# Batch 1's values half pooled on VectorE, five normalisations on ScalarE, and a new order of steps in a pooled-attention and MLP-mixer kernel

## The chip, the cores and the metric

The kernel runs on one core of a Trainium2 chip. The core has a matrix engine (TensorE, in the profile PE, with its weight loads as PEld), a vector engine (VectorE, DVE), a scalar engine (ScalarE, ACT), GpSimd (POOL) and SyncE (SP), which work side by side, each through its own instructions in order, and wait for each other by semaphores. TensorE writes its products to PSUM, from where DVE or ACT fetches them. The metric is the time of one execution on the device in microseconds (us), median of several runs.

## The reference

Attention over pooled keys and values, then an MLP mixer. There are 8 batches, 8 heads, 576 positions, 64 elements a head.

```python
k_p = k.reshape(B, H, 72, 8, D).mean(axis=3)        # 8 neighbours pooled: 72 keys
v_p = v.reshape(B, H, 72, 8, D).mean(axis=3)
scores = scale * q @ k_p^T                          # 576 x 72 a head
attn = exp(scores) / sum(exp(scores))
x = (attn @ v_p), heads side by side                # (8, 576, 512)
h = relu(x^T @ w_tok1) @ w_tok2                     # 576 -> 256 -> 576
u = x + h^T
out = u + relu(u @ w_ch1) @ w_ch2                   # 512 -> 1536 -> 512
```

## The kernel before

The kernel is one long program whose order is written out by hand. HEAD is a string of steps that load and compute batch 0 up to the mixer's input. PLAN has a dictionary for each of nine **units**. A unit n is the channel MLP (w_ch1, relu, w_ch2, sum) of the first 512 rows of batch n; the ninth (n = 8) does the remaining 64 rows of all eight batches together. A unit is a generator (unit_fast) that stops 45 times, at steps 0 to 44, each after about 0.44 us of matmuls; PLAN says which steps of the later batches are put in at each stop. So the MLP of batch n and the attention of batches n+1 to n+3 share TensorE.

The steps of a batch b are written "b.name" (functions in batch_steps):
- lk, lq, lv load the keys, queries and values (POOL's DMA queue); s0 to s2 compute scores and their exponentials (TensorE, then ACT).
- K0, K1 and V0, V1 pool half of the keys or values by three additions on POOL (pool8, L173 to L183). k0, k1, v0, v1 do the same on DVE, vpool0 and vpool1 by eight identity matmuls on TensorE (ppool, L261) and a copy.
- Q0, Q1 transpose the queries (DVE); kpT transposes the pooled keys on TensorE, with a copy on ACT.
- av0 to av4 multiply the exponentials with the values for one block of rows (TensorE, L388), take the reciprocal of the sums (DVE, L392) and normalise: one multiplication on DVE (L331). With on_act, named aw0 to aw4, the reciprocal stays on DVE and the normalisation is eight ACT multiplications, one a head, each with a scale of its own per row (L333 to L335).
- at0, at1 are the token MLP's first product, u0 to u4 its second with the sum x + h (L423); t0 to t3 transpose u through TensorE and ACT. From batch 3 on the transposition goes through memory instead: M0, M2, M4 write u out, M and MT read it back in another layout (SP's queue), T0 to T5 transpose blocks on DVE (L465).

Steps without a batch: "=1" to "=4" are sums of parts of the hidden activations GT (g_sums, DVE), w0 to w3 sums of w_ch2 (weight_sum). "g" is a gate: DVE writes a flag (L809) and POOL copies it (L810), so that POOL does not go on to its later loads and poolings before DVE is there. In HEAD, d1 to d4 are dummy matmuls on TensorE, p0 and p1 permute w_tok2 (ACT, POOL), c0 and c1 convert queries, Lxx are loads.

The MLP in a unit. In units 0 to 6 twelve l1_tile calls (L523, two steps each) make GT with a relu on ACT (L530). In units 7 and 8 (FAST) l1_fast makes it in 21 smaller products of three groups A, B, C, seven each, in the order of ORDER; ACT keeps partial products (L621), DVE adds them (L625) and applies the relu (L628). Then seven products of twelve matmuls (product, L680) make the output, each three steps, with additions on DVE (L723). Before the change, in a FAST unit, the first product starts when all 21 are issued and three empty steps have gone by.

PSUM has four banks of one tile, p1a to p1d, handed out in turn (take, give), and two double buffers p2 that scores and av share.

Of the kernel before, what the change touches and what calls it, by code (L numbers as in the profile page):

```python
# [12 lines left out]
ALU = mybir.AluOpType  # L13
# [8 lines left out]
PLAN = [  # L22
# [9 lines left out]
]  # L32

# [2 lines left out]
def kernel(  # L36
# [523 lines left out]

    def g_sums(s, eng):
        S4 = sums_tile("S", "area")
        if s[0] == "3":
            sub(S4[:, 2], GT[:, 0, f], GT[:, 1, f], eng)
        elif s[0] == "1":
            eng.tensor_tensor(out=S4[:, 0], in0=GT[:, 1, f], in1=GT[:, 1, sec], op=ALU.add)
        elif s[0] == "2":
            sub(S4[:, 1], S4[:, 0], GT[:, 0, f], eng)
        else:
            sub(S4[:, 3], GT[:, 0, sec], S4[:, 1], eng)  # L570

    def weight_sum(k):
        T = sums_tile("T", "area2")
# [28 lines left out]
    def l1_fast(n, uT):  # L602
# [20 lines left out]
        def add(g, k, ps, row, half):  # L623
            dst = GT[:, half, row * NH + 2 * g:row * NH + 2 * g + 2]
            nc.vector.tensor_tensor(out=dst, in0=ps, in1=kept[g, k], op=ALU.add)  # L625
            if g > 0:
                dst = GT[:, half, row * NH + 4 * (g - 1):row * NH + 2 * g + 2]
                nc.vector.tensor_scalar(out=dst, in0=dst, scalar1=0.0, scalar2=None, op0=ALU.max)  # L628

        def step(g, k):  # L630
            if k == 1:
                if g > 0:
                    bank[g, 0], bank[g, 1] = (take([P, 2, 256], FP32) for _ in range(2))
                else:
                    bank[g, 0], bank[g, 1] = (ps_two.tile([P, 2, 512], FP32, name="p2")[:, 0].rearrange(
                        "p (j n) -> p j n", j=2) for _ in range(2))
            ps = bank[g, k in (2, 3, 5)]
            a, c = factors[k]
            for j in range(2):
                for kk in range(2):  # L640
                    nc.tensor.matmul(out=ps[:, j], lhsT=a(2 * g + j, kk), rhs=c(kk),
                                     start=k in (1, 2, 5) and j == 0 and kk == 0, stop=kk == 1, skip_group_check=True)
            if k == 1 or k == 5:
                keep(g, k)
            elif k == 6:
                keep(g, 2)
            elif k == 2:
                add(g, 1, ps, 0, 0)
            elif k == 3:
                add(g, 2, ps, 0, 1)  # L650
            elif k == 7:
                add(g, 5, ps, 1, 1)
            else:
                nc.scalar.activation(out=GT[:, 0, NH + 2 * g:NH + 2 * g + 2], in_=ps, func=AF.Relu)
                if g == NM // 4 - 1:
                    for i in range(4):
                        give(bank[1 + i % 2, i // 2])

        return step

    ORDER = "A1 A2 B1 B2 A6 C1 C2 A5 A7 B6 A3 B5 B7 A4 C6 B3 C5 C7 B4 C3 C4"

    def unit_fast(n, u):
        last = n == B
        uT = [u["uT"][:, kk, :] for kk in range(4)]
        if n in FAST:
            step = l1_fast(n, uT)
            for t in ORDER.split():
                step("ABC".index(t[0]), int(t[1]))
                yield  # L670
            for _ in range(3):
                yield
        else:
            for m in range(NM):
                yield from l1_tile(n, m, uT)

        def product(ps, a, w, start, after, split=False, end=None):
            for i in range(2):
                for m in range(NH):
# [45 lines left out]
                    then(e)  # L725
            return go

        def store_part(cols, engines):
            def go(i):
                if len(engines) == 2:  # L730
                    engines[i].dma_start(out=tail_rows(1, cols)[:, i], in_=ob[:, i, cols])
                elif i == 1:
                    engines[0].dma_start(out=tail_rows(1, cols), in_=ob[:, :, cols])
# [4 lines left out]
        x, y = bank(last), bank()  # L738
        s1 = keep("s1")
        yield from product(x, lambda m: GT[:, 0, m], lambda m: w_ch2[:, m, lo], True,  # L740
                           plus(part(s1), part(x), residual(0, 0)), last)
# [142 lines left out]
```

## Time and profile before

| | |
|---|---|
| median of 3 runs | 264.78 us (264.6 to 265.11) |
| the profiled execution | 265.02 us |
| its span, first to last instruction | 263.2 us |
| instructions | 5488 |
| granted TensorE clock, mean | 0.999 |
| HBM read, written | 38.99 MB, 12.58 MB (196 GB/s over the span) |

The span cut at the handovers from one unit to the next, roughly (us of busy time of each engine):

| stretch, us | what | PE | DVE | ACT | POOL |
|---|---|---|---|---|---|
| 24 to 57 | unit 0 | 32.03 | 25.42 | 15.89 | 18.28 |
| 57 to 87 | unit 1 | 29.10 | 22.06 | 19.49 | 28.79 |
| 87 to 115 | unit 2 | 27.63 | 20.48 | 13.06 | 25.31 |
| 115 to 146 | unit 3 | 29.93 | 25.31 | 13.31 | 26.55 |
| 146 to 222 | units 4 to 6 | 75.73 | 52.74 | 33.50 | 46.19 |
| 222 to 241 | unit 7 | 18.87 | 18.38 | 6.86 | 2.98 |
| 241 to 263 | unit 8 and the end | 18.51 | 18.07 | 6.86 | 0.00 |

How to read lines of the timeline: start and length in us, engine, line of the kernel, operation, tile written <- tiles read, shape, how many are merged (x); in brackets the idle time of that engine before it, and what ended it. Starts count from the first instruction. Matmuls are pipelined, so the length of one is more than its spacing to the next: a matmul of 512 columns follows the one before it after 0.216 us, one of 256 after 0.109.

### The profile page before, as it was taken

How to read it: one execution, taken by the hardware profiler on the slowest of the kernel's cores; microseconds unless marked ns; L12 is line 12 of the kernel's file. 1: busy time of each engine (PE TensorE's matmuls, PEld its weight loads, DVE VectorE, ACT ScalarE, POOL GpSimd, SP SyncE). 2: the span in 40 equal slices, each digit the busy share in tenths (PEclk: the TensorE clock that was granted, in tenths of full speed). 3: DMA queues.
4: the chain of work that ended last, by engine and by line, in shares of the span. 5: the costliest groups of instructions: out<-in, count | busy, mean ns of one | idle time of the engine just before them, and what ended most of it. 6: DMA issues, size and time to landing. Idle time of an engine off the chain costs nothing. (4 is left out here: it accounts for less than half of the span.)

```text
span 263.2 us, 5488 instructions
## 1 busy us (share of the span) xinstructions
PE 254.0 (97%) x2171; PEld 167.7 (64%) x2193; DVE 195.7 (74%) x400; ACT 119.0 (45%) x195; POOL 166.1 (63%) x177
## 2 busy tenths in 40 slices
PE   8999999989999999999998999999999999999994
PEld 2785466754667544774476447754684478888883
DVE  3557469986787665896599686863696389999994
ACT  2355763149537466415640565255625421712700
POOL 8667326899999999978879992798407922100000
PEclk9999999999999999999999999999999999999999
DMA  7999999993079928599645932650315052602404
GB/s 148 187 198 207 205 207 208 206 225 75 4 127 145 163 86 168 133 185 249 127 152 94 215 130 66 97 156 1 126 37 161 2 157 63 181 0 49 114 2 159
DMA packets 31706, 34.31 MB, mean 130 GB/s; under 512 B 3136, under 2 KB 23744, under 8 KB 31680
## 3 DMA queue, kind: packets, MB, share of 16 engines
q0 software_dynamic: 17632, 17.64, 42.4%
q1 hardware_dynamic: 13632, 15.93, 20.4%
q8 instruction: 17, 0.28, 0.5%
q10 hardware_dynamic: 416, 0.39, 0.5%
q14 instruction: 9, 0.07, 0.1%
HBM read 38.99 MB, written 12.58 MB: 196 GB/s over the span
## 5 line engine op out<-in xcount | busy, mean ns | idle before, releaser
L526 PEld LDWEIGHTS <-w_ch 128*128 128x128 bf16 x336 | 30.2, 98 | 33.4 <-issue 2.7
L680 PEld LDWEIGHTS <-area 128*128 128x128 bf16 x432 | 41.4, 98 | 7.5 <-issue 1.0
L810 POOL COPY flag<-flag 1x1 f32<-1x1 f32 x41 | 12.5, 304 | 43.1 <-DVE flag L809 43.0
L309 ACT ACTIVATE ex<-p 72x768 bf16<-72x768 f32 x42 | 31.5, 802 | 17.1 <-PE p L300 17.1
L680 PEld LDWEIGHTS <-GT 128*128 128x128 bf16 x324 | 30.7, 98 | 7.5 <-issue 1.6
L178 POOL TENSOR_TENSOR t<-t 72x512 f32<-72x512 f32 x23 | 32.4, 1409 | 1.8
L526 PE MATMUL p1c<-uT,w_ch 128*128 128x512 bf16 x100 | 28.0, 379 | 0.2
L177 POOL TENSOR_TENSOR t<-kr 72x1024 f32<-72x1024 bf16 x12 | 25.5, 2121 | 0.4
L177 POOL TENSOR_TENSOR t<-vr 72x1024 f32<-72x1024 bf16 x11 | 23.4, 2123 | 2.4 <-DMA vr<-in_v_dram 1.9
L331 DVE TENSOR_TENSOR x<-p,den 128x512 bf16<-128x512 f32 x32 | 22.1, 691 | 1.1
L526 PE MATMUL p1b<-uT,w_ch 128*128 128x512 bf16 x75 | 21.3, 379 | 0.4 <-issue 0.2
L530 ACT ACTIVATE GT<-p1c 128x512 bf16<-128x512 f32 x26 | 15.5, 597 | 12.3 <-PE p1c L526 8.5
L526 PE MATMUL p1a<-uT,w_ch 128*128 128x512 bf16 x72 | 20.5, 379 | 0.3
L526 PE MATMUL p1d<-uT,w_ch 128*128 128x512 bf16 x74 | 19.9, 379 | 0.2 <-issue 0.2
L530 ACT ACTIVATE GT<-p1b 128x512 bf16<-128x512 f32 x20 | 11.9, 596 | 15.3 <-PE p1b L526 8.8
L530 ACT ACTIVATE GT<-p1d 128x512 bf16<-128x512 f32 x19 | 11.4, 599 | 14.0 <-PE p1d L526 8.5
L388 PEld LDWEIGHTS <-ex 72*128 72x128 bf16 x280 | 12.9, 98 | 7.5 <-DVE x L331 2.0
L423 DVE TENSOR_TENSOR u<-p1d,x 128x512 bf16<-128x512 f32 x11 | 8.0, 727 | 11.9 <-PE p1d L422 11.0
L554 DVE TENSOR_TENSOR area<-GT 128x1536 bf16<-128x1536 bf16 x9 | 11.4, 1263 | 6.9 <-ACT AT L402 5.2
L388 PE MATMUL p<-vp,ex 72*128 72x65 bf16 x280 | 14.4, 194 | 1.0 <-DVE x L331 0.5
L121 POOL DMA_DIRECT2D kr<-in_k_dram x17 | 10.9, 646 | 5.4 <-PE p1c L526 2.0
L680 PE MATMUL p1a<-area,area 128*128 128x256 bf16 x108 | 14.3, 273 | 0.0
(235 smaller groups left out, 536.6 us busy)
## 6 DMA issues: line engine op xcount, KB each, us to landing
out_dram<-o SPq DMA_DIRECT2D x32, 256.0 KB, 4.1
qb<-in_q_dram POOLq DMA_DIRECT2D x7, 576.0 KB, 10.3
kr<-in_k_dram POOLq DMA_DIRECT2D x7, 512.0 KB, 8.9
vr<-in_v_dram POOLq DMA_DIRECT2D x7, 512.0 KB, 14.4
w_ch<-in_moe_w_ch_dram POOLq DMA_DIRECT2D x5, 512.0 KB, 14.5
mem<-u SPq DMA_DIRECT2D x10, 256.0 KB, 2.2
v<-mem SPq DMA_DIRECT2D x20, 128.0 KB, 2.9
area<-in_q_dram SPq DMA_DIRECT2D x2, 288.0 KB, 3.0
```

What stands on the lines that cost most here:

```text
L121: nc.gpsimd.dma_start(out=t[j0:j1, h0:h1].rearrange("j h i d -> j h (i d)"), in_=src[b, h0:h1].rearrange("h (j i) d -> j h (i d)", i=POOL) ...
L177: eng.tensor_tensor(out=t4[:, 0:n], in0=t[:, hs, 0:4], in1=t[:, hs, 4:8], op=ALU.add)
L178: eng.tensor_tensor(out=t4[:, 0:n, 0:2], in0=t4[:, 0:n, 0:2], in1=t4[:, 0:n, 2:4], op=ALU.add)
L309: nc.scalar.activation(out=dst, in_=src, func=AF.Exp, scale=scale)
L331: nc.vector.tensor_tensor(out=dst, in0=view, in1=den[:, :, :, None].broadcast_to([n, a, 4, D]), op=ALU.mult)
L388: nc.tensor.matmul(out=ps[:, h // 4, (h % 4) * (D + 1):(h % 4 + 1) * (D + 1)], lhsT=st["ex"][:, h * S + n0:h * S + n0 + P], rhs=st["vp"][: ...
L423: nc.vector.tensor_tensor(out=rows_of(c), in0=blocked(ps), in1=blocked(x), op=ALU.add)
L526: nc.tensor.matmul(out=ps, lhsT=w_ch1[:, kk, m * P:(m + 1) * P], rhs=uT[kk], start=(kk == 0), stop=(kk == 3))
L530: nc.scalar.activation(out=GT[:, :, m, :], in_=ps.rearrange("p (h n) -> p h n", h=2), func=AF.Relu)
L554: eng.tensor_tensor(out=out, in0=a, in1=b, op=ALU.subtract)
L680: nc.tensor.matmul(out=ps[i] if split else ps[:, i], lhsT=chunk(u, i, a(m)), rhs=w(m), start=start and m == 0 and (i == 0 or split), stop= ...
L810: nc.gpsimd.tensor_copy(out=flag[:, 1:2], in_=flag[:, 0:1])
```

## The change

In HEAD: the loads, the dummies and some steps stand in another order, with 20 dummy matmuls instead of 19; 0.u1, 0.u0, 1.kpT and 1.Q1 move from unit 0 to the end of HEAD.

In PLAN: the steps of units 0 to 3 are laid out anew. In unit 0, 1.vpool1 (TensorE) becomes 1.v1 (DVE), and av0, av2 and av4 of batch 1 become aw; in unit 1 2.av3 and in unit 3 5.av3 become aw. Units 4, 5, 6 and 8 stay; in unit 7 7.Y3 moves from step 12 to step 0.

In units 7 and 8: the first output product is cut into three parts X and put between the last products of group C; banks go back to the pool as soon as group B or C is through; the relu of group B goes from DVE to POOL. In the last unit the addition to the output after the second product waits until the third one's addition is done. Group sums can be cut in halves (not used in the plan), and the last store is written otherwise with the same stores.

```diff
-HEAD = """LkA LkT LkB LvT Lq LvA LvB Lt1 Lk1 Lt2 Lc1b Lc1a Lq1 Lc1c Lv1 Lc1d p1 Lc2a Lc2b Lc2c d2 d2 d3 d1 d4 d4 c0 c1 prep q0 kp0 kp1 kt0 q1 d1 o0 kt1 kp2 e0 e1 q3 kt2 o1 q2 e3 vpool0 o3 e2 a00 vpool1 a02 o2 m01 d1 d1 m00 a04 X1 m03 a14 m02 X0 m04 p0 a10 a12 1.kpool m10 m14 m12 m13 m11 A1 A0 X2 X3 A2 A3"""
+HEAD = """LkT LkA LkB LvT Lq LvA LvB Lt1 Lk1 Lt2 Lc1a Lc1b Lq1 Lc1c Lv1 p1 Lc1d Lc2b Lc2a d2 d1 d2 d1 Lc2c d3 c0 d4 d4 c1 prep q0 kp0 kp1 kt0 q1 d1 kt1 o0 kp2 e0 q3 kt2 o1 e1 q2 e3 vpool0 o3 e2 a00 vpool1 a02 o2 m01 d1 d1 a04 X1 a14 m02 m03 m00 X0 m04 p0 a10 a12 1.kpool m10 m14 m13 m12 m11 A1 A0 X3 A3 X2 A2 0.u1 0.u0 1.kpT 1.Q1"""
 PLAN = [
-    {0: "2.lk 0.u1 1.kpT 1.Q0 1.Q1", 3: "0.u0 3.lq 2.lq", 6: "1.s0 0.u2", 8: "g", 9: "0.u3 1.s1", 10: "1.vpool1 2.lv", 12: "1.s2 1.vpool0", 13: "=3", 14: "1.av1 1.av2", 17: "1.av0", 18: "1.av4 g", 19: "w0", 20: "3.lv 1.av3", 22: "w1", 23: "g =1 =2", 24: "3.lk", 25: "=4", 26: "1.at0 g", 27: "2.K0", 28: "w3 1.at1", 30: "g", 31: "1.u2", 32: "2.K1", 33: "1.u0 2.V0", 34: "1.u1", 35: "w2", 37: "1.t2", 40: "1.u3", 41: "1.t0", 42: "1.t3", 43: "1.t1 2.Q0 1.u4", 44: "g 2.kpT 2.Q1 3.Q0"},
-    {1: "2.v1 2.s0", 4: "3.K0", 8: "3.K1 2.s2", 11: "g", 12: "2.s1", 15: "3.Q1", 16: "2.av3", 17: "4.lq 2.av1", 18: "4.lk", 19: "2.av0", 20: "2.av4", 23: "2.av2 =1 g", 25: "2.at0 =2", 26: "g", 27: "3.kpT", 28: "2.at1 =4", 31: "2.u3", 32: "3.s2 4.Q1", 33: "2.u2", 34: "5.lk", 35: "3.s0", 36: "3.V1 =3", 37: "2.t3", 39: "3.s1 3.V0 4.lv g 2.u0", 41: "2.u1 2.t2", 42: "2.t0 g", 43: "2.t1 3.av0", 44: "3.av4"},
-    {2: "3.av2", 4: "4.K1", 6: "4.K0 3.av1", 7: "3.av3", 11: "3.at1", 12: "g", 13: "3.at0", 15: "=3", 17: "4.Q0 3.u1 4.kpT", 18: "6.lk 3.u3 4.V1 3.u0", 20: "3.u2 4.s2", 21: "3.u4 3.M0", 23: "4.V0 g", 24: "3.M2", 25: "=1", 26: "5.lq 4.s0", 27: "=2", 28: "g", 29: "=4 6.lq", 30: "4.s1 3.M", 32: "3.T3", 33: "5.lv 3.T0", 35: "g", 36: "4.av1 g", 37: "3.M4 3.T2 3.T1", 38: "6.lv", 40: "g", 41: "3.MT", 43: "4.av2", 44: "4.av4"},
-    {3: "5.K1 4.av0", 5: "4.av3 5.K0", 7: "6.Q0", 8: "4.at1", 10: "4.at0 g", 11: "5.Q1", 12: "5.Q0", 13: "3.T4", 15: "3.T5 5.kpT 4.u3 4.u2 4.u1", 16: "5.V1 g", 17: "5.s0", 18: "=3", 20: "4.u0", 24: "5.s1", 25: "=1 4.M0 4.M2", 26: "=2 =4", 28: "5.V0 5.s2 g", 30: "g", 32: "5.av0 7.lq", 35: "5.av2", 36: "5.av1 4.M", 40: "5.av4 5.av3", 41: "4.T0", 42: "4.T1 4.T3", 43: "4.T2 5.at0 5.at1"},
+    {0: "2.lk 1.Q0", 1: "0.u2", 3: "3.lq 2.lq", 4: "g", 5: "1.v1 1.s0", 9: "1.s1", 11: "0.u3", 12: "1.s2 1.vpool0", 13: "1.aw0 =3", 14: "2.lv 1.av1", 16: "1.aw2", 17: "1.av3 g", 20: "w0 1.aw4 w1 g", 21: "3.lv 3.lk", 22: "w3", 23: "=1 =2", 26: "1.at1", 27: "=4", 28: "g 1.at0 2.K0", 32: "g", 33: "1.u1 1.u2", 34: "1.u0", 35: "w2", 36: "1.t2 2.K1", 38: "1.t0", 39: "g 2.V0", 41: "1.u3 2.Q1", 43: "1.t1 1.t3 1.u4 2.Q0", 44: "2.kpT"},
+    {0: "2.s0", 1: "3.K1", 5: "2.s2", 9: "2.s1 2.v1", 12: "3.Q0", 14: "g", 15: "2.av1", 17: "2.av4 3.K0", 18: "2.av0", 19: "4.lq", 22: "4.lk", 23: "2.aw3 2.av2", 24: "g", 25: "2.at0 =1 3.Q1 =2", 28: "=4 3.kpT", 29: "2.at1 3.s2", 30: "2.u2 2.u0", 32: "5.lk 2.u3", 34: "3.V0", 35: "3.V1 =3", 36: "2.t0 3.s0", 37: "g", 39: "2.t3", 40: "3.s1 g 2.u1", 41: "4.lv", 42: "2.t2 3.av2", 43: "2.t1 3.av0"},
+    {1: "4.K1", 6: "3.av1", 7: "3.av3", 9: "3.av4", 10: "3.at0 4.Q0 4.K0 3.at1", 13: "4.Q1 4.V1 3.u0 3.u2 4.kpT", 15: "4.s1 6.lk g", 17: "4.V0 3.u1 3.u3", 21: "3.M0", 23: "4.s2 g 3.u4", 24: "3.M2", 25: "=1", 26: "4.s0", 27: "5.lq =3", 28: "=2 g", 29: "3.M", 30: "=4", 33: "3.T3 6.lq", 34: "5.lv 3.T0 g", 36: "g", 37: "6.lv 3.M4", 39: "3.T2 4.av1 3.MT", 41: "3.T1", 42: "g", 43: "4.av4 4.av2"},
+    {1: "4.av0", 2: "5.K1", 5: "4.av3 5.K0", 7: "3.T5 4.at1 4.at0", 9: "g", 10: "5.Q1", 12: "5.Q0", 14: "4.u2", 15: "3.T4 4.u3 5.kpT", 17: "6.Q0 5.s0 5.V1", 18: "=3", 20: "g", 21: "4.u1", 23: "4.u0", 24: "5.s1", 25: "4.M2 =1", 27: "=2", 28: "4.M0 5.V0", 29: "=4 7.lq 5.s2 g", 31: "5.av0 g", 32: "5.av2", 33: "4.M", 36: "5.av1", 38: "5.aw3", 40: "5.av4", 42: "4.T3 4.T2 4.T0", 43: "5.at0 4.T1", 44: "5.at1"},
...
-    {0: "g", 6: "7.MT", 12: "7.Y3", 18: "g", 21: "=1", 27: "=2", 30: "=3", 32: "=4", 34: "7.T4", 35: "7.T5", 40: "8.y0", 41: "8.y1 8.y3", 42: "8.y2"},
+    {0: "g 7.Y3", 6: "7.MT", 18: "g", 21: "=1", 27: "=2", 30: "=3", 32: "=4", 34: "7.T4", 35: "7.T5", 40: "8.y0", 41: "8.y1 8.y3", 42: "8.y2"},
@@ l1_fast
-                nc.vector.tensor_scalar(out=dst, in0=dst, scalar1=0.0, scalar2=None, op0=ALU.max)
+                (nc.vector if g > 1 else nc.gpsimd).tensor_scalar(out=dst, in0=dst, scalar1=0.0, scalar2=None, op0=ALU.max)
...
-                if g == NM // 4 - 1:
-                    for i in range(4):
-                        give(bank[1 + i % 2, i // 2])
+                if g > 0:
+                    give(bank[g, 1])
+                    give(bank[g, 0])
...
-    ORDER = "A1 A2 B1 B2 A6 C1 C2 A5 A7 B6 A3 B5 B7 A4 C6 B3 C5 C7 B4 C3 C4"
+    ORDER = "A1 A2 B1 B2 A6 C1 C2 A5 A7 B6 A3 B5 B7 A4 C6 B3 C5 C7 B4 C3 X C4 X X"
@@ unit_fast
+            for t in ORDER.split():
+                if t != "X":
+                    step("ABC".index(t[0]), int(t[1]))
+                    yield
+                    continue
+                if first is None:
+                    x = bank(last)
+                    first = product(x, *first_args(x))
+                next(first)
+                yield
...
+        first_cols = plus(cols_of(oa, 0), part(y), part(s1))
         yield from product(y, lambda m: GT[:, 0, NH + m], lambda m: w_ch2[:, NH + m, lo], True,
-                           plus(cols_of(oa, 0), part(y), part(s1)), end=y)
+                           (lambda e: None) if last else first_cols, end=None if last else y)
...
+        def fifth(e):
+            plus(part(s5), part(z), residual(1, 1))(e)
+            if last:
+                first_cols(e)
+                give(y)
...
-        yield from product(z, lambda m: SG[:, 0, m], lambda m: TW[:, 0, m], True,
-                           plus(part(s5), part(z), residual(1, 1)))
+        yield from product(z, lambda m: SG[:, 0, m], lambda m: TW[:, 0, m], True, fifth)
```

More of the change, by code (lines that the diff above doesn't have):

```diff
@@ L562, in g_sums @@
         S4 = sums_tile("S", "area")
+        m0, m1 = {"": (0, NH), "a": (0, 4), "b": (4, NH)}[s[1:]]
+        S = [S4[:, i, m0:m1] for i in range(4)]
+        g = [[GT[:, half, r * NH + m0:r * NH + m1] for r in range(2)] for half in range(2)]
         if s[0] == "3":
-            sub(S4[:, 2], GT[:, 0, f], GT[:, 1, f], eng)
+            sub(S[2], g[0][0], g[1][0], eng)
         elif s[0] == "1":
-            eng.tensor_tensor(out=S4[:, 0], in0=GT[:, 1, f], in1=GT[:, 1, sec], op=ALU.add)
+            eng.tensor_tensor(out=S[0], in0=g[1][0], in1=g[1][1], op=ALU.add)
         elif s[0] == "2":
-            sub(S4[:, 1], S4[:, 0], GT[:, 0, f], eng)
+            sub(S[1], S[0], g[0][0], eng)
         else:
-            sub(S4[:, 3], GT[:, 0, sec], S4[:, 1], eng)
+            sub(S[3], g[0][1], S[1], eng)
     def weight_sum(k):
@@ L654, in step @@
                 nc.scalar.activation(out=GT[:, 0, NH + 2 * g:NH + 2 * g + 2], in_=ps, func=AF.Relu)
-                if g == NM // 4 - 1:
-                    for i in range(4):
-                        give(bank[1 + i % 2, i // 2])
+                if g > 0:
+                    give(bank[g, 1])
+                    give(bank[g, 0])
         return step
-    ORDER = "A1 A2 B1 B2 A6 C1 C2 A5 A7 B6 A3 B5 B7 A4 C6 B3 C5 C7 B4 C3 C4"
+    ORDER = "A1 A2 B1 B2 A6 C1 C2 A5 A7 B6 A3 B5 B7 A4 C6 B3 C5 C7 B4 C3 X C4 X X"
     def unit_fast(n, u):
         last = n == B
[L665 to L675, printed above, removed]
         def product(ps, a, w, start, after, split=False, end=None):
@@ L726, in plus, with store_part @@
             return go
-        def store_part(cols, engines):
+        def store_part(cols):
             def go(i):
[L730 to L733, printed above, removed]
-            return go
+                if i == 1:
+                    nc.scalar.dma_start(out=tail_rows(1, cols), in_=ob[:, :, cols])
+            return go
@@ new lines, in first_args @@
+        def first_args(x):
+            return (lambda m: GT[:, 0, m], lambda m: w_ch2[:, m, lo], True, plus(part(s1), part(x), residual(0, 0)), last)
+        s1, first = keep("s1"), None
+        uT = [u["uT"][:, kk, :] for kk in range(4)]
+        if n in FAST:
+            step = l1_fast(n, uT)
+            for t in ORDER.split():
[8 more added lines that the diff above has]
+                yield
+            for _ in range(3):
+                yield
+        else:
+            for m in range(NM):
+                yield from l1_tile(n, m, uT)
@@ L736, in unit_fast @@
         SG, TW = sums_tile("S", "area"), sums_tile("T", "area2")
         oa, ob = (outp.tile([P, 2, DM], FP32, name="o") for _ in range(2))
[L738 to L741, printed above, removed]
+        if first is None:
+            x = bank(last)
+            yield from product(x, *first_args(x))
+        y = bank()
+        first_cols = plus(cols_of(oa, 0), part(y), part(s1))
@@ L760, in unit_fast @@
             yield from product(x, lambda m: SG[:, 2, m], lambda m: TW[:, 2, m], False,
-                               plus(cols_of(ob, 1), part(x), part(s5), store_part(hi, [nc.scalar])), True)
-            yield from product(x, lambda m: GT[:, 1, NH + m], lambda m: TW[:, 3, m], False,
-                               plus(cols_of(ob, 0), part(x), residual(1, 0), store_part(lo, [nc.scalar, nc.sync])), True)
+                               plus(cols_of(ob, 1), part(x), part(s5), store_part(hi)), True)
+            r = residual(1, 0)
+            for i in range(2):
+                for ks in (slice(0, 2),):
+                    cols = slice(ks.start * P, ks.stop * P)
+                    for m in range(NH):
+                        nc.tensor.matmul(out=x[i][:, cols], lhsT=chunk(u, i, GT[:, 1, NH + m]), rhs=TW[:, 3, m, cols],
+                                         start=False, stop=(m == NH - 1), skip_group_check=True)
+                    view = [v.rearrange("p (k a f) -> p k a f", a=4, f=D // 2) for v in (ob[:, i, cols], x[i][:, cols])]
+                    nc.vector.tensor_tensor(out=view[0], in0=view[1], in1=r(i)[:, ks], op=ALU.add)
+                (nc.sync if i else nc.scalar).dma_start(out=tail_rows(1, lo)[:, i], in_=ob[:, i, lo])
+                yield
         else:
```

## The prediction

> **What bounds the kernel now.** I read the page first (busy time, slices), then the table of waits, then the timelines of PE, DVE, ACT and POOL around each place where PE's matmuls start later than their spacing allows.
>
> ```profile
> PE 254.0 (97%) x2171; PEld 167.7 (64%) x2193; DVE 195.7 (74%) x400; ACT 119.0 (45%) x195; POOL 166.1 (63%) x177
> ```
>
> PE has something in work for 254.0 of 263.2 us. Of the remaining 9.2 us, 1.19 lie ahead of the first matmul and 3.5 behind the last (PE ends at 259.7). Some 4.5 us of holes are all that a new order can win, beside PE work that is really removed. The table of waits says whom PE waits for:
>
> ```profile
> PE p1c L225 <- POOL kp L181: 1.1, 1, 1.1
> PE p L388 <- DVE x L331: 0.5, 1, 0.5
> PE p L345 <- ACT ex L325: 0.4, 1, 0.4
> PE p L388 <- POOL vp L183: 0.4, 2, 0.2
> ```
>
> The longest hole stands at the end of unit 0: kpT of batch 2 waits for the keys that POOL pools (K0, then K1). The timelines of PE, POOL and DVE show what sets it:
>
> ```profile
> 57.33 0.24 PE L225 MATMUL p1c<-ident,kp 72*128 72x72 bf16 x2 [1.08 <-POOL kp L181]
> ...
> 43.17 0.95 DVE L566 TENSOR_TENSOR area<-GT 128x1536 bf16<-128x1536 bf16 x1
> ...
> 46.65 0.06 DVE L809 MEMSET flag<- 1x1 f32 x1
> ...
> 46.80 0.83 POOL L810 COPY flag<-flag 1x1 f32<-1x1 f32 x1 [0.76 <-DVE flag L809]
> 47.59 2.12 POOL L177 TENSOR_TENSOR t<-kr 72x1024 f32<-72x1024 bf16 x1
> ...
> 56.44 0.83 POOL L181 TENSOR_TENSOR kp<-t 72x256 bf16<-72x256 f32 x1
> ```
>
> K0 and K1 keep POOL from 47.59 to 57.27 without a hole; K0 starts behind a gate (L809/L810), the gate stands on DVE behind the sums, and the first sum ("=1") starts at 43.17, after the last relu of the unit (ACT, ended 42.12). So the start of unit 1 hangs on ACT's last relu, through DVE and POOL. By the starts of its matmuls PE loses there 1.24 us; at the handover from unit 1 to 2 0.36+0.12+0.17+0.26 = 0.9; late in unit 3 0.36+0.68+0.15 = 1.2; and in units 7 and 8 0.29 each, where C4 waits for the add of C7:
>
> ```profile
> 230.30 0.60 PE L641 MATMUL p1d<-uT,vr 128*128 128x256 bf16 x4
> 231.03 0.60 PE L641 MATMUL p1c<-qb,w_ch 128*128 128x256 bf16 x4
> ...
> 230.28 0.69 DVE L625 TENSOR_TENSOR GT<-p1c,ex 128x512 bf16<-128x512 f32 x1
> ```
>
> C3 starts at 230.30 and needs 0.44; C4 starts 0.29 later than that, when DVE has read bank p1c.
>
> **Part 1: head and unit 0.** PE loses the eight matmuls of 1.vpool1 (32.07 to 32.94: 0.87) and gains one dummy (0.22 apart once the clock is up, 0.43 before): I take -0.87+0.22 = -0.65, range -0.65 to -0.4. The moved u1, u0, kpT and Q1 keep their order to within two matmuls and cost nothing: their inputs are old by then. In their place DVE gets 1.v1. Its row is 2.v1 in unit 1: 1.69+1.64+0.84, begun at 58.87 and done at 63.1, beside POOL's own pooling; alone I put it at 2.2 to 4.2. It starts when the values have landed, about 30 us by the bytes ahead of them in POOL's DMA queue, at some 0.2 MB a us. It is done by 34; DVE was two thirds idle from 28 to 35, and behind it are only u3 and the copy of vpool0, wanted from 34.6 on. So nothing, or 0.3 if the copy is late.
>
> The three normalisations aw0, aw2, aw4 are the weighty edit. Each takes 0.69 from DVE and puts eight multiplications of 128x64 on ACT. No such row exists. Nearest: two relus of 128x512 start 0.47 apart (30.40, 30.87), and a pass of 256 costs 0.38 against 0.60 for 512, so 0.16 fixed plus 0.86 ns an element. Eight fully overlapped cost 8x0.1+0.15 = 0.95; eight without overlap 8x0.21 = 1.7; and eight cannot cost more than eight of 256, 3.0. I take 1.7, the line through the single rows, since nothing shows overlap for passes as short as these.
>
> ```profile
> 30.40 0.59 ACT L530 ACTIVATE GT<-p1c 128x512 bf16<-128x512 f32 x1
> 30.87 0.60 ACT L530 ACTIVATE GT<-p1a 128x512 bf16<-128x512 f32 x1
> ```
>
> The Trainium skill, "ScalarE: Activation LUTs", What ACT_TABLE_LOAD costs, gives 186 ns + 0.833 ns an element, 93 more for a per-partition operand and 93 of overlap between neighbours: an estimate of 8x0.24+0.09 = 2.0 for eight, by which the whole sum would be about 0 instead of -1.15. The same page of the Trainium skill, Rules for kernel authors, puts multiplications on VectorE altogether, which speaks against this edit; no trace here shows one on ACT.
>
> Now the path. vpool0 ends on PE at 34.6, aw0's matmuls run at 35.3 behind the copy of the values, its reciprocal (0.2) and then ACT from 36.0 to 37.7. There are two p2 buffers, so aw2 needs aw0's: due at 37.1, it waits until 37.75. aw4 needs aw2's, read out at 40.2, and is due at 40.0. ACT is in order: relus of tiles 7, 8, 9 stand between, aw4 ends at 42.9, and relus 10 and 11 behind it at 43.9. "=1" starts at 43.95 instead of 43.17, the gate behind =1, =2, the first add and =4 fires 3.48 later as before, at 47.4, and K0 starts at about 47.6 (the copy of the gate was held for 0.83 beside a DVE sum; now an add from PSUM stands there). So K1 ends near 57.3 as before, PE arrives somewhat later than 56.06 and waits the rest: **term 0.0**. At 0.95 a set all of the stalls fall away, the gate fires near 45.5, K1 ends at 55.0 and PE comes through at 55.6: -1.7. Above 1.7 every 0.1 us counts three times, +0.3.
>
> **Part 2: unit 1 and the handover to unit 2.** 2.aw3 stands two steps ahead of at0, whose fourth matmul reads its result: matmuls 0.26, reciprocal 0.25, ACT 1.7, against 1.8 of PE work between. **+0.4** (0 to 1.3, by the same price). POOL's V1 and V0 of batch 3 stood behind two gates and two key loads (start 77.18, end 86.45, av0 waited at 86.51); now V0 is behind one gate and may start near 75, so that hole closes, and the four later normalisations are spread wider than DVE's 0.9 each: **-0.9** (-0.9 to 0). 2.t1 now has 0.7 of PE work behind it, not 0.96, against about 0.85 for its copy: **+0.15**.
>
> **Part 3: units 2 and 3.** "=3" of unit 2 moves into the stage where DVE has no hole (105.33 to 119.9), and T1 of batch 3 goes behind an add of the output: 0.95+0.65+0.65 more ahead of T1, less 0.77 that DVE waited for POOL. T1 ends at about 115.7 instead of 114.2; unit 3's first matmul is due at 115.5. **+0.3** (0 to 1.5). In unit 3 ACT idles for 9 us while DVE is full:
>
> ```profile
> 144.94 0.60 ACT L402 ACTIVATE AT<-p1b 128x512 bf16<-128x512 f32 x1 [9.01 <-PE p1b L400]
> ```
>
> 5.aw3 lies in that idle time and takes 0.6 from DVE; av2 comes earlier and av1 no longer queues right behind av0. The wait for V0 at 136.4 stays (POOL waits for its load before). **-0.5** of the 1.2 (-1.2 to +0.3). 3.T5 moves ahead of Q1 and Q0 and its data landed only at about 123.2: DVE is held some 3 us there, but s0 needs Q0 only at 126.8, so it costs nothing unless the landing slips by 1.5.
>
> **Part 4: units 7 and 8.** X between C3 and C4 fills the 0.29 in both: in unit 7 **-0.3** stands whole, since its banks are given back earlier and its later sums have 0.85 of slack. In unit 8 DVE runs without a hole from 242.9 to 258.2, and the same ten operations stand between "=1" and the last add but two; only "=1" itself comes earlier, by 0.3, since the relus of group B no longer stand on DVE ahead of C3's add. So **-0.3** again, and not the 0.29+0.23 that PE alone would give. The relus of group B move to POOL: DVE's 0.43 against 1.15 for a POOL pass over two inputs of 128x512, the same number of elements read, up to 2.3 at the rate of the 128x576 copy (1.26). "=1" needs the last one about 2.1 after the add: at 1.3 it is there, at 2.3 unit 8 loses 0.65 and gives its gain away. The Trainium skill, "GPSIMD Engine Reference", 4.1 Engine selection, calls one-input work roughly line rate there, an estimate of 0.9 us at its 1.2 GHz, by which the term stands; no trace here shows it.
>
> Sum: 0.0+0.4-0.75+0.3-0.5-0.6 = **-1.15 us**. The profiled execution took 265.02 (span 263.2 and 1.8 around it), 0.24 over the median of 264.78. So 263.87 on its scale, **263.6** on the median's.
>
> **The rivals.** (a) *Cheap multiplications*: at 0.95 a set unit 0 gives -1.7 and unit 1's +0.4 falls: -3.25, 261.5. For it: the 0.47 spacing of relus. Against: every multiplication carries its own operand, which no row has. (b) *ACT becomes the bound*, slower: three sets delay the last relu of unit 0, hence "=1", the gate, K0, K1 and kpT, by three times what a set costs over 1.7, and aw3 adds it once more. The point from which it decides is 1.7+1.15/4 = 2.0 a set: there the sum is 0 (264.8), beyond it the kernel is slower, at 2.5 by 4x0.8-1.15 = +2.05, 266.8. For it: strict order on ACT, the two p2 buffers, and a chain with no slack behind it. Against: the line through the single rows gives 1.7, and the pairs less. (The figures of the Trainium skill above, "ScalarE: Activation LUTs", put a set just at that point.) (c) *The handovers eat it*: T1 late by its 1.5 rather than 0.3, unit 3 without its gain: -1.15+1.2+0.5 = +0.5 at worst, about 264.8 in the middle. For it: DVE full at the end of unit 2. Against: DVE's own wait of 0.77 may shrink further.
>
> **Chances.** Forecast 0.41, (a) 0.20, (b) 0.25, (c) 0.14. This kernel's measurement tells about 0.2% (0.5 us) from no change. Forecast and (a) are faster; of (b) 0.06 is same and 0.19 slower; of (c) 0.03 is faster, 0.06 same and 0.05 slower. So faster 0.64, same 0.12, slower 0.24. The range from 261.4 (a) to 266.2 leaves out the worse half of (b) and little else.
>
> **What would show it.** Right: eight ACT passes of about 0.21 each per aw; K0 starting near 47.6; no wait of PE on vp near 86; C4 right behind X in unit 7. Wrong: K0 near 45.5 (a) or past 49 (b); PE waiting at the first matmul of unit 3 for more than 1 us (c); "=1" of unit 8 waiting for POOL.

## The result, and the profile after

The changed kernel is slower: 274.97 us median (273.09 to 278.56, 4 executions) against 264.69 (264.33 to 265.11, 4 executions) on the same chip, a ratio of 1.0364 (95% interval 1.0266 to 1.0462). Ratios, here and below, leave out executions that took over 1.5% more than the fastest of their kernel, here the one of 278.56. The forecast was 263.6, its range ended at 266.2. The profiled execution took 273.09, with a span of 271.3 us. The page of the changed kernel, part 1:

```profile
PE 256.5 (95%) x2186; PEld 166.6 (61%) x2186; DVE 193.9 (71%) x390; ACT 126.6 (47%) x235; POOL 179.0 (66%) x182
```

PE is busy for 2.5 us more and the span is 8.0 longer, so most of the loss is holes. To find them I cut both traces where each unit's first MLP matmul starts:

| | unit 1 starts | unit 1 | unit 2 | unit 3 | units 4 to 6 | unit 7 | unit 8 to PE's end |
|---|---|---|---|---|---|---|---|
| before, us | 57.40 | 30.06 | 28.07 | 30.73 | 75.71 | 18.66 | 19.08 |
| after, us | 57.91 | 32.45 | 29.73 | 29.76 | 75.71 | 20.57 | 21.61 |
| difference | +0.5 | +2.4 | +1.66 | -0.96 | 0 | +1.9 | +2.5 |

The differences add to 8.0. The +0.5 ahead of unit 1 can't be told from the variation of the head: over the traces of all kernels below, PE begins the work on the first keys (L235) anywhere from 7.46 to 8.89 us, in ten of the fourteen after a wait for their landing; with the old head and unit 0 as it was, unit 1 starts between 57.15 and 58.54, with the new head and unit 0 between 57.65 and 58.53. The waits of PE in the changed kernel (us in total, times, longest) name the other places:

```profile
PE p1c L422 <- DVE o L714: 1.7, 1, 1.7
PE p1a L671 <- DVE area L569: 1.5, 1, 1.5
PE p1b L671 <- DVE area L569: 1.4, 1, 1.4
PE p1b L671 <- DVE flag L837: 1.3, 1, 1.3
```

None of these four is in the table of before. L569 is "=1", in units 7 and 8; L422 is u in unit 1; L837, a gate's flag, is only the last DVE instruction ahead of what PE really waits for, at the end of unit 2.

**Unit 7.** Timelines of POOL, DVE and PE of the changed kernel:

```profile
232.39 5.53 POOL L631 TENSOR_SCALAR GT<-GT 128x1024 bf16<-128x1024 bf16 x2 [0.88 <-DVE GT L628]
...
237.95 0.96 DVE L569 TENSOR_TENSOR area<-GT 128x1536 bf16<-128x1536 bf16 x1 [1.61 <-POOL GT L631]
...
234.32 0.60 PE L671 MATMUL p1c<-w_ch,GT 128*128 128x256 bf16 x4
...
238.97 1.49 PE L671 MATMUL p1b<-area,area 128*128 128x256 bf16 x12 [1.43 <-DVE area L569]
```

One relu on POOL takes 2.77 us, and two stand back to back; "=1" could have started at 236.34 (237.95 less its wait of 1.61), and PE waits for it. The hole of 0.29 ahead of C4 is gone: X fills it. Unit 8 repeats this, with 0.24 and 0.3 us more of waits for a sum (DVE s L714).

**Unit 1.** The same three engines, and below them "=4" in the kernel before:

```profile
73.58 0.38 PE L400 MATMUL p1a<-x,w_tok 128*128 128x512 bf16 x1 [0.48 <-ACT x L335]
...
75.48 3.69 DVE L554 TENSOR_TENSOR area<-GT,area 128x1536 bf16<-128x1536 bf16 x1
...
76.21 2.14 POOL L177 TENSOR_TENSOR t<-vr 72x1024 f32<-72x1024 bf16 x1
...
79.82 0.59 PE L422 MATMUL p1c<-AT,w_tok 128*128 128x512 bf16 x2 [1.68 <-DVE o L714]
```

```profile
74.99 0.95 DVE L554 TENSOR_TENSOR area<-GT,area 128x1536 bf16<-128x1536 bf16 x1 [0.57 <-DVE s L723]
```

The first line is 2.aw3 on ACT holding at0 (0.64 by the starts of the matmuls). The second is "=4": 3.69 us where before it took 0.95. It ends at 79.17, 0.82 after POOL's first addition of V0 (78.35). Behind it on DVE stands the addition that frees PE's bank; PE loses 1.84 by its starts. These two, less a hole of 0.36 that went, are 2.1 of the +2.4.

**Unit 2.** POOL's load of 5.lq, SP's issue of the read-back M, the transposition T3 and T0 on DVE, and PE:

```profile
106.71 0.76 POOL L131 DMA_DIRECT2D qb<-in_q_dram  x1
...
109.23 1.80 SPq L453 DMA_DIRECT2D v<-mem  x4
...
115.91 0.77 DVE L465 STREAM_TRANSPOSE uT<-v 128x256 uint32<-128x256 uint32 x2 [2.62 <-DMA v<-mem]
...
117.36 1.03 PE L671 MATMUL p1b<-area,area 128*128 128x256 bf16 x8 [1.29 <-DVE flag L837]
```

In before, M was issued first, the load 2.0 us behind it, and T3 started at 111.33 without a wait:

```profile
106.87 1.80 SPq L453 DMA_DIRECT2D v<-mem  x4
...
108.89 0.75 POOL L131 DMA_DIRECT2D qb<-in_q_dram  x1
```

Now the load goes first, and DVE waits 2.62 us for the read-back. By the starts of its matmuls PE loses 1.45, 0.65 and 0.24 there, while 0.55 of holes at the start of the unit are gone.

### The profile page after: what moved, and what is told of

Same layout as the page of the kernel before. It is cut to its first block, busy times and chain, and to the rows that moved or that the text cites. A ratio compares the mean times of both kernels' runs of the same rounds, so it can differ in the third digit from the quotient of the medians.

```text
span 271.3 us, 5541 instructions
## 1 busy us (share of the span) xinstructions
PE 256.5 (95%) x2186; PEld 166.6 (61%) x2186; DVE 193.9 (71%) x390; ACT 126.6 (47%) x235; POOL 179.0 (66%) x182
## 5 line engine op out<-in xcount | busy, mean ns | idle before, releaser
L671 PEld LDWEIGHTS <-area 128*128 128x128 bf16 x432 | 40.8, 98 | 13.8 <-DVE area L569 3.5
L838 POOL COPY flag<-flag 1x1 f32<-1x1 f32 x40 | 10.6, 264 | 47.0 <-DVE flag L837 46.9
L631 POOL TENSOR_SCALAR GT<-GT 128x1024 bf16<-128x1024 bf16 x6 | 16.6, 2777 | 13.2 <-DVE GT L628 13.2
L526 PE MATMUL p1b<-uT,w_ch 128*128 128x512 bf16 x92 | 24.0, 379 | 0.0
L526 PE MATMUL p1d<-uT,w_ch 128*128 128x512 bf16 x88 | 23.6, 379 | 0.0
L526 PE MATMUL p1a<-uT,w_ch 128*128 128x512 bf16 x84 | 22.7, 379 | 0.1
L530 ACT ACTIVATE GT<-p1b 128x512 bf16<-128x512 f32 x23 | 13.8, 602 | 14.5 <-PE p1b L526 9.0
L530 ACT ACTIVATE GT<-p1a 128x512 bf16<-128x512 f32 x21 | 12.6, 600 | 16.7 <-PE p1a L526 16.6
L331 DVE TENSOR_TENSOR x<-p,den 128x512 bf16<-128x512 f32 x28 | 19.4, 692 | 1.0
L526 PE MATMUL p1c<-uT,w_ch 128*128 128x512 bf16 x72 | 19.5, 379 | 0.0
L671 PE MATMUL p1b<-area,area 128*128 128x256 bf16 x120 | 15.2, 273 | 2.7 <-DVE area L569 1.4
L569 DVE TENSOR_TENSOR area<-GT 128x1536 bf16<-128x1536 bf16 x9 | 9.7, 1077 | 8.0 <-ACT GT L530 4.8
L554 DVE TENSOR_TENSOR area<-GT 128x1536 bf16<-128x1536 bf16 x9 | 10.6, 1183 | 5.6 <-ACT AT L402 5.2
```

Source lines behind the costliest of these rows:

```text
L331: nc.vector.tensor_tensor(out=dst, in0=view, in1=den[:, :, :, None].broadcast_to([n, a, 4, D]), op=ALU.mult)
L526: nc.tensor.matmul(out=ps, lhsT=w_ch1[:, kk, m * P:(m + 1) * P], rhs=uT[kk], start=(kk == 0), stop=(kk == 3))
L530: nc.scalar.activation(out=GT[:, :, m, :], in_=ps.rearrange("p (h n) -> p h n", h=2), func=AF.Relu)
L554: eng.tensor_tensor(out=out, in0=a, in1=b, op=ALU.subtract)
L569: eng.tensor_tensor(out=S[0], in0=g[1][0], in1=g[1][1], op=ALU.add)
L631: (nc.vector if g > 1 else nc.gpsimd).tensor_scalar(out=dst, in0=dst, scalar1=0.0, scalar2=None, op0=ALU.max)
```

## The experiments

Twelve kernels, each with the full computation. Of PLAN the diffs show the changed entries of one unit only. "The changed kernel with ..." starts from after, the others from before. Every ratio is against before on the same chip (medians 264.31 us for the first four experiments, 264.61 for the next four, 264.41 for the last four). Theory: three collisions (POOL's relu, "=4" with V0, 5.lq with M), each a wait that can be taken away by itself. Rivals: the ACT normalisations, as the prediction's rival (b) had it, or a general loss by the new order.

**The changed kernel with the relus of group B on DVE:**

```diff
-                (nc.vector if g > 1 else nc.gpsimd).tensor_scalar(out=dst, in0=dst, scalar1=0.0, scalar2=None, op0=ALU.max)
+                nc.vector.tensor_scalar(out=dst, in0=dst, scalar1=0.0, scalar2=None, op0=ALU.max)
```

> The changed kernel with one line undone: the relu of group B goes back from POOL to DVE. Theory (each POOL relu takes 2.77 us, two stand back to back, and "=1" waits 1.6 us for the last one in units 7 and 8): both waits go, unit 7 falls from 20.6 to about 18.4 us and unit 8 with the end by about 2.5 to 3, the whole by some 4.5 to 5 us, to 268 to 270. Rival (the interleaved product X itself is at fault, because it shortens the cover between C4 and the sums): the waits before the third product stay above 1 us and less than 2 us are won.

272.13 (269.06 to 275.57), ratio 1.0237 (1.0181 to 1.0293); profiled 269.06. Units 7 and 8 are 18.48 and 19.40 us: 4.3 of the 8.0 belong to the POOL relu. (Whole profiled executions differ by 4.0, medians by 2.8.)

**Before with only the relus of group B on POOL** (the same edit, the other way):

> The kernel before with that one line alone: group B's relu on POOL, everything else as before. Theory: the same two POOL passes back to back hold "=1" in units 7 and 8 although the products are in the old order; 3 to 4 us slower, 268 to 269. Rival (only together with the interleaved X is it harmful): within 0.7 us of before.

274.06, ratio 1.0351 (1.0315 to 1.0386). Worse than expected: units 7 and 8 took 25.23 and 21.39 us, and the clock was at half for 3.41 us from 233.49 on. POOL's timeline and PE's in unit 7:

```profile
229.14 2.77 POOL L628 TENSOR_SCALAR GT<-GT 128x1024 bf16<-128x1024 bf16 x1 [0.92 <-DVE GT L625]
...
233.08 0.66 PE L641 MATMUL p<-qb,w_ch 128*128 128x256 bf16 x4 [4.91 <-POOL qb L554]
```

7.Y3, an addition on POOL that PE needs, stands behind the relu; in the changed kernel it is at step 0, ahead of it, and no such wait is there. That move, to which I gave no term, keeps the new relu from costing more; by how much no run of the move alone tells.

**Before with only the overlap X** and what goes with it (banks given back early, the late addition in unit 8), the relus on DVE:

```diff
-    ORDER = "A1 A2 B1 B2 A6 C1 C2 A5 A7 B6 A3 B5 B7 A4 C6 B3 C5 C7 B4 C3 C4"
+    ORDER = "A1 A2 B1 B2 A6 C1 C2 A5 A7 B6 A3 B5 B7 A4 C6 B3 C5 C7 B4 C3 X C4 X X"
```

> HEAD and PLAN of before with the changed MLP code (X between C3 and C4, banks returned early, the later addition in the last unit), but the relu of group B on DVE. Theory of the prediction: 0.3 us won in unit 7 and 0.3 in unit 8, 264.1. Rival: DVE sets the end of both units and nothing is won (264.7), or the later addition costs in unit 8 (265 or more).

264.97, ratio 1.0013 (0.9991 to 1.0035): no change. Unit 7 gains 0.18, unit 8 loses 0.33, in one wait for a sum.

**Before with only unit 3's new line:**

```diff
-    {3: "5.K1 4.av0", 5: "4.av3 5.K0", 7: "6.Q0", 8: "4.at1", 
...
+    {1: "4.av0", 2: "5.K1", 5: "4.av3 5.K0", 7: "3.T5 4.at1 4.at0",
...
```

> The kernel before with the line of unit 3 alone from the change (5.aw3 and the new order there). Theory: unit 3 took 29.77 us in the changed kernel against 30.73, so this line alone gives about -0.9: 263.8. Rival: unit 3 was shorter only because unit 2 ended late and gave POOL and DVE a lead; then it gives nothing or costs some tenths.

264.67, ratio 1.0001 (0.9975 to 1.0028): no change. Unit 3 took 30.29 us; with its old line it took from 29.72 to 30.94 in the traces of the other kernels. So the -0.96 of the result is no gain of the line.

**The changed kernel with DVE relus and unit 1's gate behind "=4",** so that V0 can't start beside it:

```diff
-    24: "g", 28: "=4 3.kpT"
+    28: "=4 g 3.kpT"
```

> e1 (relu of group B on DVE) with one gate moved in unit 1: from step 24 to behind "=4" in step 28, so that POOL starts the key load and V0 of batch 3 only when DVE is through "=4". Theory ("=4" took 3.69 us instead of 0.95 because it met POOL's V0, and PE waited 1.84 us for the add behind it): "=4" takes about 0.95 again, unit 1 falls from 32.4 us to about 30.6 and the whole by some 1.8. Rival (DVE is late at that place anyway, or the wait turns up behind V0, at the first products of unit 2): less than 0.7 us won. If this wait is also what drops TensorE's clock in some executions, the spread of e1 (269.1 to 275.6) shrinks as well.

277.91, ratio 1.0481 (1.0435 to 1.0528). In unit 1 "=4" is as expected:

```profile
75.20 0.95 DVE L554 TENSOR_TENSOR area<-GT,area 128x1536 bf16<-128x1536 bf16 x1
```

"=4" takes 0.95 again, and the unit is 1.2 shorter (31.22), not 1.8: POOL's next pooling now meets "=3", which takes 2.92 us at 82.00, and PE waits 0.6 for the addition behind it. Unit 2 grew to 39.56, and T3 waits about 12 us for the read-back. This is the third collision, much enlarged. The trace shows how: DVE has u ready sooner, so SP issues its transfer to memory (mem<-u, 102.54) 0.8 us behind POOL's load of 6.lk (101.70), where with the DVE relus alone it was 3.1. Its second part takes 7.2 us to land instead of 4.5, M is issued only when it has landed (110.43), and by then POOL's loads for batches 5 and 6 are being issued, from 1.6 ahead of M on.

**The changed kernel with DVE relus and 5.lq behind the read-back:**

```diff
-    27: "5.lq =3", 28: "=2 g"
+    27: "=3", 28: "=2 g 5.lq"
```

> e1 with the query load 5.lq of unit 2 moved from step 27 to behind the gate of step 28, so that it is issued about 4.6 us later. Theory (the load's 0.55 MB were put on the shared DMA engines 2.5 us ahead of the read-back M of batch 3, whose data T3 then waited 2.6 us for, with PE's banks behind it): the read-back lands some 2.5 us earlier, PE's 1.45+0.65+0.24 us of waits in unit 2 fall below 1 us, and unit 2 goes from 29.4 to about 27.8. Rival (T1 stands behind too many DVE operations, as the prediction had it): the wait stays and moves to the first matmul of unit 3.

269.01 (267.51 to 274.71), ratio 1.0133 (1.0078 to 1.0188). SP and DVE:

```profile
110.11 1.80 SPq L453 DMA_DIRECT2D v<-mem  x4
...
114.50 0.77 DVE L465 STREAM_TRANSPOSE uT<-v 128x256 uint32<-128x256 uint32 x2 [0.68 <-DMA v<-mem]
```

The load is issued at 111.94, 1.8 after M. M has landed at 114.37; with the DVE relus alone it was 116.08, though M was issued 0.3 sooner there. Unit 2: 27.80 instead of 29.40 (28.07 in before). Unit 3 gives 0.4 of it back (30.20 instead of 29.76). In span this trace is still 2.8 longer than that of before: 2.4 of it are unit 1, 1.0 the later start of unit 1, and the other units are 0.6 shorter.

**Both moves together** (both diffs):

> e1 with both moves, of the gate in unit 1 and of the load in unit 2. Theory: the two are separate and add up, 3 to 3.5 us under e1's profiled 269.1, that is 265.5 to 266, with a spread like before's (2 us) since no stall of more than 1.3 us is left. Rival: something in units 0 to 3 is still unnamed and the median stays above 267.

278.14, ratio 1.0506 (1.0464 to 1.0547). POOL, SP and DVE, and the granted clock in the page's 40 slices:

```profile
110.54 1.48 POOL L131 DMA_DIRECT2D qb<-in_q_dram  x2
...
111.23 2.04 SPq L453 DMA_DIRECT2D v<-mem  x4
...
125.13 0.77 DVE L465 STREAM_TRANSPOSE uT<-v 128x256 uint32<-128x256 uint32 x2 [12.71 <-DMA v<-mem]
```

```profile
PEclk9999999999999999955999999999999999999999
```

One load is issued 0.7 ahead of M (110.54), a second 0.06 behind M's first part, a third 0.8 behind it, and M's four parts take a median of 10.3 us to land. PE then stands idle for 11.4 us, and the clock is granted at half from 118.69 to 132.34. So the two moves aren't additive. With the gate moved, the transfer of u out is again only 0.9 behind 6.lk and M late (111.23), and the load behind the gate of step 28 no longer comes behind M.

**Before with 1.v1 in step 5 and av0, av2, av4 as aw:**

```diff
-    6: "1.s0 0.u2", 10: "1.vpool1 2.lv", 14: "1.av1 1.av2", 17: "1.av0", 18: "1.av4 g"
+    5: "1.v1", 6: "1.s0 0.u2", 10: "2.lv", 14: "1.av1 1.aw2", 17: "1.aw0", 18: "1.aw4 g"
```

> The kernel before with the first half of the title alone, in unit 0: 1.vpool1 becomes 1.v1 (step 5) and av2, av0 and av4 of batch 1 become aw2, aw0, aw4 at their own steps; nothing else moves. Theory of the prediction: eight ACT multiplications take 1.75 us, the last relu of unit 0 comes later, "=1" and the gate with it, and what TensorE saves (0.87) is spent waiting for K1: within 0.7 us of before, with the wait at kpT of batch 2 longer than 1.24. Rival: the two edits are what slows the changed kernel down, 2 us or more.

271.45, ratio 1.0233 (1.0191 to 1.0275). Unit 0 took 39.26 us, not 33.08. DVE and PE:

```profile
31.79 1.22 DVE L177 TENSOR_TENSOR t<-vr 72x1024 f32<-72x1024 bf16 x1 [3.67 <-DMA vr<-in_v_dram]
...
34.87 1.34 PE L526 MATMUL p1d<-uT,w_ch 128*128 128x512 bf16 x4 [3.11 <-DVE flag L809]
```

v1 waits 3.67 us on DVE for the values to land; the additions of u2 and u3, which free banks, are queued behind it. PE stops for 3.1 us, and the clock is at half from 35.44 to 38.85. The next two kernels take the two edits apart, with v1 at another place.

**Before with aw0, aw2, aw4 alone:**

```diff
-    14: "1.av1 1.av2", 17: "1.av0", 18: "1.av4 g"
+    14: "1.av1 1.aw2", 17: "1.aw0", 18: "1.aw4 g"
```

> The kernel before, with batch 1's normalisations 0, 2 and 4 on ScalarE instead of VectorE (three of the five), batch 1's value pooling left on GpSimd, and every other step where it was. My theory: eight ScalarE multiplications take about 1.75 us where VectorE took one operation; TensorE then waits twice for the buffer of batch 1's attention weights (0.5 to 1 us each time), the relu of unit 0's group, the addition "=1" and through it the K pooling of batch 2 (gate in step 26) start later, and the wait for the pooled K at the end of unit 0 grows; 266.2 to 267.2 profiled, unit 0 34.5 to 35.5 us long instead of 33.08. The rival, that TensorE's order has enough other matmuls to hide it: within 0.5 us of before.

266.83 (265.96 to 267.83), ratio 1.0085 (1.0059 to 1.0111), profiled 267.83: slower, by a little more than I expected; unit 0 35.64 us, the other units as in before. (Batch 1's value pooling stays on TensorE here, not on GpSimd.) PE:

```profile
39.90 0.42 PE L388 MATMUL p<-vp,ex 72*128 72x65 bf16 x8 [0.74 <-ACT x L335]
...
42.52 0.42 PE L388 MATMUL p<-vp,ex 72*128 72x65 bf16 x8 [1.33 <-ACT x L335]
```

The waits for the double buffer p2 are there, as in rival (b) and in my theory. "=1" starts at 45.85 instead of 43.17, K0 at 50.28 instead of 47.59, unit 1 at 59.98 instead of 57.40: the chain through relu, sums, gate and K pooling passes the delay on whole.

**Before with v1 alone, behind the additions:**

```diff
-    10: "1.vpool1 2.lv"
+    10: "1.v1 2.lv"
```

> The kernel before, with the half of batch 1's value pooling on VectorE, but in step 10, behind the additions of unit 0's u2 and u3, and not in step 5 ahead of them; the normalisations as before. My theory: the pooled values on VectorE by themselves cost nothing once no addition that TensorE needs for a free bank stands behind them: no wait of 3 us for a bank, no half clock, unit 0 33 us (within 0.5), the time within 0.5 us of before. The rival, that 2.3 us of extra VectorE work hold TensorE wherever they stand: 1 to 3 us slower, as in the run with the pooling in step 5 (unit 0 34 to 36 us).

263.33 (262.73 to 264.39), ratio 0.9958 (0.9940 to 0.9977): 0.4% faster than before, small but outside the interval. Unit 0 took 32.37 us, 0.71 less. DVE:

```profile
31.16 0.73 DVE L423 TENSOR_TENSOR u<-p1b,x 128x512 bf16<-128x512 f32 x1 [0.99 <-PE p1b L422]
31.79 1.20 DVE L177 TENSOR_TENSOR t<-vr 72x1024 f32<-72x1024 bf16 x1
```

The pooling starts with no wait, 0.63 after u3 began, and lies beside PE work. My theory of "no change" fell: I had thought the wait for K1 would eat the 0.87 of PE. But the gate hangs on ACT's last relu, hence on PE itself; when PE gets there earlier, K0 starts earlier too (46.87, not 47.59). Unit 3, too, was 0.98 shorter in this trace than in that of before, and also in others with the same line: late in unit 3 of before PE waits 0.19 us for pooled values and 0.52 for a normalisation, and in the short ones it doesn't. Why stays open, so not all of the 1.08 us between the medians need be v1's.

**Before without the gate of step 26 in unit 0:**

```diff
-    26: "1.at0 g"
+    26: "1.at0"
```

> The kernel before without the gate of step 26 in unit 0, so that GpSimd begins batch 2's K pooling about 1.5 us earlier. One theory: the wait for the pooled K at the end of unit 0 (1.24 us in before) goes, 1.0 to 1.3 us faster (263.5), unit 0 about 31.9 us long. The other, which the collision of unit 1's "=4" with GpSimd's value pooling in the changed kernel suggests: the K pooling now runs beside VectorE's two-input sums ("=4", w3) and one holds the other, so that a sum that took 1 us takes 2 to 4 us, and TensorE waits there what it gains at the end: no change (within 0.4 us) or up to 1.5 us slower.

264.47, ratio 1.0008 (0.9986 to 1.0030): no change. POOL, DVE and PE:

```profile
46.56 2.15 POOL L177 TENSOR_TENSOR t<-kr 72x1024 f32<-72x1024 bf16 x1
...
47.25 2.28 DVE L554 TENSOR_TENSOR area<-w_ch,area 128x1536 bf16<-128x1536 bf16 x1
...
50.18 0.59 PE L422 MATMUL p1b<-AT,w_tok 128*128 128x512 bf16 x2 [1.12 <-DVE flag L809]
```

PE no longer waits for kpT (the row is gone from its waits) but waits 1.12 here: w3 takes 2.28 beside K0's first addition and not 0.95, and ends 0.82 after that addition. The second theory holds: the same collision as "=4" with V0, made on purpose in another place. Unit 0 took 33.15 us against 33.08. (Units 1 and 2 are 0.36 and 0.34 shorter in this trace, unit 8 0.2 longer; the medians show no gain.)

**Before with the overlap, the first columns' addition left where it was:**

```diff
-                           (lambda e: None) if last else first_cols, end=None if last else y)
+                           first_cols, end=y)
```

> The kernel before with the overlap of the first matrix product with the last group of unit 7 and 8 alone (relus on VectorE as before), and in unit 8 the addition into the first columns left behind its own product instead of one product later. The run with the changed order had 0.18 us less in unit 7 and 0.33 us more in unit 8. If the late addition is what costs the 0.33, unit 8 is now 19.0 or less and the time 0.2 to 0.4 us under before (264.4); if it is not, unit 8 is again 19.3 to 19.4 us and the time that of before.

264.23, ratio 0.9989 (0.9970 to 1.0007): no change. Unit 7 took 18.48 us and unit 8 19.22 instead of 19.41. So the late addition may be half of what unit 8 lost, but this isn't shown: unit 8 with the code of before took 19.07 to 19.08 in four traces and 19.28 and 19.29 in two, so 19.22 in one trace is inside its variation. A wait of 0.36 for a sum is left:

```profile
254.79 1.47 PE L671 MATMUL p1d<-w_ch,area 128*128 128x256 bf16 x12 [0.36 <-DVE s L714]
```

## Why the prediction was wrong, point by point

**"The relus of group B move to POOL ... at 1.3 it is there"** (Part 4): this step failed, and it is the largest. The relu took 2.77 us. My 1.3 leaned on a two-input addition of the same number of elements read (1.15), my upper bound of 2.3 on the rate of a copy of 128x576 (1.26); the relu took more for each element it read than either. I also looked at one relu alone: its input was there at 234.56, so by itself it would have ended at 237.3, 1.0 late; behind the one before it, it ended at 237.92, 1.6 late. The sum had -0.6 for units 7 and 8; it was +4.4, and DVE relus took back 4.3. At 2.3 I had priced only 0.65 in unit 8, for one relu. The estimate from the Trainium skill, "GPSIMD Engine Reference", 4.1 Engine selection (0.9 us), was three times too low. The closing of the hole by X was right in unit 7, at -0.18 in place of -0.3; in unit 8 it gave no gain even alone, where PE then waits 0.33 for a sum of DVE.

**"Now V0 is behind one gate and may start near 75, so that hole closes: -0.9"** (Part 2): V0 did start earlier (76.21 instead of 77.18), and PE's waits at the handover to unit 2 went. I counted the earlier start as a gain only, and did not look at what ran on DVE at that moment. "=4" had kept clear of POOL's pooling in before, because a gate stood between. The term of -0.9 became +1.84 less the handover's 0.9; taking the collision away gave 1.2 back. 2.aw3 cost 0.64 where I had 0.4.

**"=3 of unit 2 moves ... T1 ends at about 115.7: +0.3 (0 to 1.5)"** (Part 3): the place was right and the mechanism wrong. I counted operations on DVE. What made T3 late was the order of two DMAs: 5.lq, moved ahead of the read-back. Moving it back took unit 2 from 29.40 to 27.80, under the 28.07 of before. For 5.lq the prediction followed no queue at all.

**"-0.5" for unit 3:** the trace shows -0.96, but the line alone measured nothing. It was right by chance.

**Unit 0, "term 0.0":** the price of a set held. The set of multiplications took 1.75 us (predicted 1.7):

```profile
36.23 1.75 ACT L335 ACTIVATE x<-p,den 128x64 bf16<-128x64 f32 x8 [0.16 <-DVE den L392]
...
44.34 0.96 DVE L569 TENSOR_TENSOR area<-GT 128x1536 bf16<-128x1536 bf16 x1 [0.80 <-ACT GT L530]
...
48.11 2.12 POOL L177 TENSOR_TENSOR t<-kr 72x1024 f32<-72x1024 bf16 x1
...
57.84 0.24 PE L225 MATMUL p1b<-ident,kp 72*128 72x72 bf16 x2 [0.84 <-POOL kp L181]
```

Predicted: "=1" at 43.95, K0 at 47.6, K1's end at 57.3; measured 44.34, 48.11 and 57.78: 0.4 to 0.5 late all along, which is less than the start of unit 0 varies between executions (25.52 to 26.39 with the new head). So the term can't be told from 0.0, nor from +0.5. The single runs show the two prices behind it in the old order, +2.6 for three normalisations and -0.7 for v1; that the new order hides the difference is argued, not shown. What I had wrong is "so nothing, or 0.3" for v1 at step 5: in the old order it cost 3.1 us of PE, because additions are queued behind it. The changed kernel escapes this: 0.u1 and 0.u0 went into HEAD and u3 behind step 5; v1 waits there too (2.82 us) without PE waiting for it.

**Rival (b)**, ACT as the bound, had the right sign and wasn't the cause: a set costs 1.75, below its point of 2.0. No rival named POOL's rate in a case of its own, DVE and POOL holding each other, or the order of DMAs. The prediction's last sign of being wrong, "=1" of unit 8 waiting for POOL, is the one that came true. Its four signs of being right came true as well (K0 0.5 late), and so didn't tell: none of them looked at the relu, at "=4" or at 5.lq.

## What to carry to other kernels

When a step moves earlier, list what else uses its engine's memory access and its DMA queue at the new time: an earlier pooling or load is a gain only if the critical operation beside it doesn't lose more. An operation that waits for a load should stand behind, not ahead of, the operations on its engine that free PE's banks; v1 ahead of them cost unit 0 3.6 us more (39.26 against 35.64), behind them it gained 0.7. And a duration on another engine is bounded by a row of that engine and that kind of operation; where there is none, the upper bound has to be wide (here the relu took 2.4 times the nearest row), and consecutive operations are to be added up.

## What the runs showed of the hardware

- **DVE and POOL hold each other.** A DVE sum of two tiles (0.95 us alone) that meets POOL's first addition of a pooling ends 0.82 after it (3.69 us in unit 1, 2.28 in the run without the gate), and POOL's next addition then takes 1.87 or 1.86 instead of 1.27. The kernel before has such meetings too (a sum of 2.53 us at 154.06, which again ends 0.82 after POOL's addition), at places where PE doesn't wait for the sum; what the change did was to put one where PE does. The Trainium skill, "SBUF — State Buffer", Who interferes with whom, says that a DVE instruction with two SBUF inputs contends with a GpSimd instruction that reads SBUF, and calls the shared port pair an exclusive lock. The trace agrees in that the sum ends only behind POOL's whole addition. What held "=4" from 75.56, the end of the operation ahead of it, to 76.21, while POOL was only issuing loads, no run here tells: beside other load issues in the same trace sums took 0.95 or 0.96 (111.74, 45.34).
- **A relu in place on POOL** (128x1024, bf16): 2.77 us, 2.7 ns an element of a row; six of them lay between 2766 and 2797 ns.
- **Queued loads and a read-back.** A read-back of four times 128 KB on SP's queue, issued 1.8 us or more ahead of POOL's next load, had landed 4.3 us after its issue (before, and with 5.lq moved back). With one load 2.5 us ahead of it, it took 6.6 (changed kernel); with loads from 1.6 or 0.7 us ahead of it on, and more while its parts were being issued, 13.0 and 13.8 (the two kernels with the gate moved).
- **The clock falls after long waits of PE.** Waits of 3.1 and 4.9 us were followed by 3.41 us at half clock; with those of 10.4 and 11.4 came 13.65, four times as long, begun while PE still waited; the profiled executions whose waits stay at 1.7 or less have none before PE's last matmul. The Trainium skill, "TensorE: Matmul & The Clock Gate", What's actually happening, gives a window of 3413 ns; the records of this case show lengths of 3413 and 13653 ns.
